# A chunk's rows of an attention and mixture-of-experts kernel: one product per pair of heads over all 128 array rows, or one per head in each half of the array rows

## The chip, the cores and the metric

The kernel runs on one core of a Trainium2 chip. The metric is the device time of one execution in microseconds (us), and smaller is better. A core has TensorE for matmuls (PE in the profile; its weight loader is PEld), VectorE (DVE), ScalarE (ACT), GpSimd (POOL) and SyncE (SP), which here issues most DMAs. TensorE multiplies a stationary operand, loaded into its array of 128 rows by 128 columns, with a moving operand whose columns stream past it. The array can be used as a whole or as smaller tiles, such as four of 64x64.

## The reference

Windowed attention for 8 batches, 8 heads, 576 positions and a head size of 64, and then a mixture of 8 experts with one expert per token:

```python
scores = scale * np.matmul(q, k.transpose(0, 1, 3, 2))
mask = (rel >= 0) & (rel < window)                       # window = 128
scores = np.where(mask, scores + bias[None], -1000000000.0)
attn = np.exp(scores - max); attn = attn / (sum + 1e-09)
x = (attn @ v) as rows of 512 per token                  # 4608 tokens
...
expert_idx = np.argmax(x @ w_gate, axis=1)               # gate: softmax's largest
out[mask] = gate_w[mask, None] * (np.maximum(xe @ w1[e], 0.0) @ w2[e])
```

All inputs and outputs are fp32. The experts' inner size is 1024.

## The kernel before

The program has two stages. The attention stage (`attention`, from line 36) goes through 36 chunks of 128 query positions each; it fills the first 200 us or so. The MoE stage (`moe_static`, line 769) gathers each expert's tokens and runs the two layers in sums of fp32r products.

A chunk is worked in these parts, which `do` (line 288) calls by a number `k`:

- `scores` (line 156), twice, for four heads each: the bias goes into two PSUM banks as bf16 matmuls (line 167), and q times k is added in fp32 (line 176). Both run in 64x64 tiles: rows are two heads, columns two halves of the queries.
- `weigh` (line 184): VectorE folds the window and takes the maxima (lines 189 and 192), ScalarE takes exponentials with their sums (line 198).
- `transposes` (line 207), twice: four fp32 transposes of 128x128 by TensorE (line 211), a copy to SBUF by ScalarE (line 213) and two masks by GpSimd (lines 221 and 223).
- `av` (line 226), twice: weights times v (line 239), in 128x64 tiles, the two heads of a pair in the two column halves; in a chunk that spans two batches a part runs in 64x64 tiles. The result is x transposed: 128 partitions are the two heads of a pair, 64 dimensions each, and the columns are 128 queries. ScalarE copies it to SBUF as `xT` (line 286).
- `rows` (line 244), once: turns x back to rows of tokens and takes the gate's logits in the same products. For each of the four pairs of heads one fp32 matmul (line 249) has `xT[:, p, :]` as the stationary operand, 128x128, and 144 columns of the constant `iw_sb` as the moving one: a 128x128 identity, and 16 columns with the pair's gate weights, 8 per head, zero where the head is the other one. The result goes to `r_ps`, two PSUM banks, two pairs in each. VectorE then multiplies by the reciprocal sums of the softmax, first the gate columns and then the rest (line 254), into `x_sb`; `done` (line 1214) adds up the logits (line 1220) and writes the rows to DRAM (line 1227).

An fp32 matmul appears in the trace as two passes, each with a weight load of its own. So the 144 row products of the program are 288 passes at line 249.

The order is written out by hand: `LAGS` gives each part of a chunk a step (4 steps per chunk), `rank` orders the parts in a step, and for the first 152 steps the engines execute in exactly that order. In a common step the second transposes of one chunk, the rows of an earlier one and the first transposes of a later one follow each other on TensorE.

`route` (line 464) works out where each token goes in its expert's list. Its small bf16 matmuls put their results in columns of `r_ps` that the rows leave free; `spare` (line 458) gives them out. The constant `iw` is built on the host (`consts`, line 1256) and loaded once (line 150).

Of the kernel before, what the change touches and what calls it, by code (L numbers as in the profile page):

```python
# [9 lines left out]
F32 = mybir.dt.float32  # L10
# [9 lines left out]
B, H, S, D = 8, 8, 576, 64  # L20
N, DM, E, F = B * S, H * D, 8, 1024
QB = 32
NP = H // 2
XW = 128 + 2 * E
SUB = 129
PITCH = 4 * SUB

# [8 lines left out]
def attention(ctx, tc, st, qT, kT, v, iw, load_c2, chunk_done, chunks, begun):  # L36
    nc = tc.nc
    const = ctx.enter_context(tc.tile_pool(name="a_const", bufs=1))
# [7 lines left out]
    ps_r = ctx.enter_context(tc.tile_pool(name="ps_r", bufs=1, space=PSUM))  # L46
# [54 lines left out]
    def make_masks():  # L101
        nc.gpsimd.memset(mask_sb, 1.0)
        for n, h in ((0, slice(0, 128)), (1, slice(0, 64)), (1, slice(64, 128))):
            nc.gpsimd.affine_select(out=mask_sb[h, n, :], in_=mask_sb[h, n, :], pattern=[[-1, 128]], base=0, channel_multiplier=1,
                                    compare_op=ALU.is_ge, fill=0.0)
    iw_sb = const.tile([128, NP, XW], F32, name="iw_sb")
    ident = st["ident"]

    warm = const.tile([128, 512], BF16, name="warm")
# [46 lines left out]
    def scores(subs, g):  # L156
        m, tail = subs[0][1] // 4, is_tail(subs)
        lo, hi = (0 if m else 128), (192 if tail else 256)
        s_ps = score_banks()
        halves = lambda c: slice(64 * c, 64 * c + 64)  # L160
        span = lambda a: (0, 192) if tail else (max(lo, 64 * a), 192 + 64 * a)
        for a in range(2):
            x0, x1 = span(a) if m else (lo, hi)
            t0 = x0 if tail else x0 - 64 * a
            for c in range(2):
                h = halves(c)
                nc.tensor.matmul(out=s_ps[halves(a), c, :, x0:x1], lhsT=eye_sb[h], rhs=bias_sb[h, 2 * g:2 * g + 2, t0:t0 + x1 - x0],
                                 start=True, stop=False)
        for n in range(2):
            for a in range(2):  # L170
                b, qs = subs[2 * a][0], slice(0, 64) if tail else halves(a)
                x0, x1 = span(a)
                k0 = 128 * (m - 1) + x0
                for c in range(2):
                    h = halves(c)
                    nc.tensor.matmul(
                        out=s_ps[halves(a), c, n, x0:x1], lhsT=blocks["q", b, m][h, 2 * g + n, qs],
                        rhs=batch[b][h, 2 * g + n, k0:k0 + x1 - x0], start=False, stop=n == 1)
        return s_ps, m, tail, lo, hi

    def guard(rsum):
        nc.gpsimd.tensor_tensor(out=rsum, in0=rsum, in1=eps_sb, op=ALU.add)
# [61 lines left out]
    def rows(ch, subs, xT, rsum):  # L244
        rinv = small.tile([128, H], F32, name="rinv")
        nc.vector.reciprocal(out=rinv, in_=rsum)
        st["r_ps"] = r_ps = ps_r.tile([128, NP, 256], F32, name="r_ps")
        for p in range(NP):
            nc.tensor.matmul(out=r_ps[:, p, 0:XW], lhsT=xT[:, p, :], rhs=iw_sb[:, p, :], start=True, stop=True)  # L249
        x_sb = xp.tile([128, NP, XW], F32, name="x_sb")  # L250
        for lo, n in ((128, E), (0, D)):
            cols = slice(lo, lo + 2 * n)
            split = lambda ap: ap[:, :, cols].rearrange("q p (c x) -> q p c x", c=2)
            nc.vector.tensor_tensor(
                out=split(x_sb), in0=split(r_ps),
                in1=rinv.rearrange("q (p c) -> q p c", c=2).unsqueeze(3).to_broadcast([128, NP, 2, n]), op=ALU.mult)
        chunk_done(ch, subs, x_sb)

# [2 lines left out]
    for ch, subs in enumerate(chunks):  # L261
        for b, i in subs:
            k = (b, i // 4)
# [6 lines left out]
    for b in range(1, B):  # L270
        at = 4 * next(ch for ch, subs in enumerate(chunks) if any(x == b for x, _ in subs))
# [10 lines left out]
    live, pes, sums, pTs, xTs, xps, second = {}, {}, {}, {}, {}, {}, {}  # L282

    def copy_x(ch):
        xTs[ch] = xp.tile([128, NP, 128], F32, name="xT", bufs=3)
        nc.scalar.copy(out=xTs[ch], in_=xps.pop(ch))

    def do(k, ch):
        if k == 9:
            return copy_x(ch)  # L290
        if k > 10:
            h = slice(4 * k - 44, 4 * k - 40)
            nc.vector.tensor_reduce(out=sums[ch][:, h], in_=pes[ch][:, h, :], axis=AX.X, op=ALU.add)
            return guard(sums[ch]) if k == 12 else None
        if k == 10:
            exps = second.pop(ch)
            exps((0,))
            copy_x(ch - 2)
            return exps((1,))
        subs = chunks[ch]  # L300
        if k in (0, 4):
            if k == 0:
                pes[ch] = pp.tile([128, H, 128], F32, name="pe")
                sums[ch] = small.tile([128, H], F32, name="rsum", bufs=8)
            live[ch] = scores(subs, k // 4)
        elif k in (2, 5):
            second[ch] = weigh(k // 3, pes[ch], sums[ch], *live.pop(ch), later=k == 5 and ch in SPLIT, add=ch not in SUMS)
        elif k == 1:
            pTs[ch] = ptp.tile([128, 2, H, 128], F32, name="pT")
            transposes(subs, 0, pes[ch], pTs[ch])  # L310
        elif k == 3:
            rows(ch, subs, xTs.pop(ch), sums.pop(ch))
        elif k == 6:
            transposes(subs, 1, pes[ch] if ch in SUMS else pes.pop(ch), pTs[ch])
        elif k == 7:
            xps[ch] = bank() if ch else ps_r.tile([128, NP, 256], F32, name="r_ps")[:, :, 0:128]
            av(subs, pTs[ch], xps[ch], range(NP // 2))
        else:
            av(subs, pTs.pop(ch), xps[ch], range(NP // 2, NP))
            if len(lags(ch)) < 10 and ch + 2 not in SPLIT:  # L320
                copy_x(ch)
# [136 lines left out]
def spare(st, k, n):  # L458
    if st["step"] >= FREE_T:
        return st["bank"]()[:, k, 0:n]  # L460
    return st["r_ps"][:, k, XW:XW + n]


def route(tc, st, lg, c0, G, groups):
# [65 lines left out]
    for k, n in enumerate(("tokh", "tokl")):  # L530
        nc.vector.tensor_tensor(out=rr[:, :, k, :], in0=eq,
                                in1=st[n][:, c0:c0 + G].unsqueeze(2).to_broadcast(sc3), op=ALU.mult)
    yield
    ip = spare(st, 1, E * TT)
    for g in range(G):
        for k in range(2):
# [132 lines left out]
def split_rows(tc, st, g, x_ps, xh, xl, gate):  # L669
    nc = tc.nc  # L670
    for d in range(4):
        nc.tensor.transpose(out=x_ps[:, d, :], in_=g[:, SUB * d:SUB * d + 128], identity=st["ident"])  # L672
    x_ps = x_ps[:, :, 0:xh.shape[2]]
# [14 lines left out]
def gather_parts(tc, st, g, idx, paced=False):  # L688
    parts = st["xd"][:, :].rearrange("t (a x) -> (t a) x", x=SUB)
    for s in range(4):  # L690
# [364 lines left out]
def moe_overflow(ctx, tc, st, w12, out):  # L1055
# [6 lines left out]
    with tc.For_i(0, n, 1) as i:  # L1062
# [15 lines left out]
        for f in range(8):  # L1078
            nc.sync.dma_start(out=w[:, f, :], in_=w12[bass.ds(e, 1), f].rearrange("o p c -> (o p) c"))
        g = op.tile([128, 4, SUB], F32, name="o_xg")  # L1080
        gather_parts(tc, st, g, idx4[:, :, 0:1])
# [112 lines left out]
def attn_moe_kernel(ctx, tc, qT, kT, v, c2, iw, w12, out):  # L1194
# [9 lines left out]
    with ExitStack() as actx:  # L1204
# [9 lines left out]
        def done(ch, subs, x_sb):  # L1214
            c0, G = next((c, n) for c, n in GROUPS if c <= ch < c + n)
            g = ch - c0
            if g == 0:
                lgs["lg"] = lgp.tile([128, G, E], F32, name="lg")
            lg = lgs["lg"]
            nc.vector.tensor_reduce(out=lg[:, g, :], in_=x_sb[:, :, 128:XW].rearrange("q p (c e) -> q e p c", c=2),  # L1220
                                    axis=AX.XY, op=ALU.add)
            for lo in (0, 2):
                if lo == 2 and subs[0][0] == subs[2][0]:
# [3 lines left out]
                nc.sync.dma_start(out=st["xd"][t0:t0 + n].rearrange("t (p x) -> t p x", p=NP),  # L1227
                                  in_=x_sb[QB * lo:QB * lo + n, :, 0:SUB])
            if g == G - 1:
# [26 lines left out]
def consts(moe_w_gate, moe_w1, moe_w2):  # L1256
    back = np.zeros((128, N // 128), np.int64)
    for ch, subs in enumerate(make_chunks()):
        for jj, (b, i) in enumerate(subs):
            back[QB * jj:QB * jj + QB, ch] = N - (b * S + QB * i + np.arange(QB))  # L1260
    wg = moe_w_gate.reshape(NP, 128, E).transpose(1, 0, 2)
    gate = np.zeros((128, NP, 2, E), wg.dtype)
    for c in range(2):
        gate[64 * c:64 * c + 64, :, c] = wg[64 * c:64 * c + 64]
    iw = np.concatenate([np.broadcast_to(np.eye(128, dtype=wg.dtype)[:, None], (128, NP, 128)), gate.reshape(128, NP, 2 * E)], axis=-1)
    parts = dict(ident=np.eye(128), seq=np.broadcast_to(np.arange(MAXOV), (128, MAXOV)), prof=np.broadcast_to(CAPS, (128, E)), rev=np.broadcast_to(np.arange(E, 0, -1), (128, E)), tokh=-64 * (back // 64), tokl=-(back % 64),
                 i128=np.broadcast_to(np.arange(128), (128, 128)), grp=np.arange(128)[:, None] // 32)
    c2 = np.concatenate([np.asarray(parts[n], np.float32) for n, _ in CONSTS], axis=1)
    w1 = moe_w1.reshape(E, 4, 4, 32, 8, 128).transpose(0, 4, 1, 3, 2, 5).reshape(E, 8, 128, 512)
    plain = moe_w1.reshape(E, 4, 128, 8, 128).transpose(0, 3, 2, 1, 4).reshape(E, 8, 128, 512)  # L1270
    w2 = moe_w2.reshape(E, 8, 128, DM)
    w12 = np.concatenate([np.concatenate([w1, w2], axis=-1), np.concatenate([plain, w2], axis=-1)])
    return dict(c2=c2, iw=iw, w12=np.ascontiguousarray(w12))
# [20 lines left out]
```

## Time and profile before

| | us |
|---|---|
| median of 3 runs | 647.56 |
| lowest and highest | 647.05, 647.61 |
| the profiled execution's own time | 646.91 |
| its span, first to last instruction | 645.2 |
| matmul passes of the rows (line 249) | 288, from 22.3 to 216.8 |

The granted TensorE clock was 0.998 of full speed over the span. How to read the views:

- A group of instructions is shown by line, engine, operation, output and inputs by name, and size: "128*64" ahead of a matmul's shapes is the rows and columns of the array that it uses, "128x144" the output's partitions and columns.
- In a timeline a row has the start in us, the time from the group's first start to its last end, the group, how many instructions, and in brackets the idle time ahead and what ended it. Matmuls overlap: the length that the trace gives for one is a latency, and the distance between starts is the pace.
- "issue" as what ended a wait means that the engine waited for nothing that the profile shows.

### The profile page before, as it was taken

What the parts mean: (1) busy time and instruction counts of PE and PEld (TensorE: products, weight loads), DVE (VectorE), ACT (ScalarE), POOL (GpSimd) and SP (SyncE); (2) the same over time, 40 slices, a digit from 0 to 9 for tenths busy, and PEclk for the clock granted to TensorE, in tenths of its full rate; (3) what the DMA queues carried; (4) which work ended last, traced back from release to release, by engine and by line L of the source; (5) the groups of instructions that cost most, each with busy time, mean ns of one, the idle gap of its engine ahead of it and who ended that gap; (6) DMA issues with size and microseconds to landing.
All of it is one profiled execution on the core that took longest, in us unless ns stands there. A gap on an engine that the chain in (4) does not pass through costs nothing.

```text
span 645.2 us, 15063 instructions
## 1 busy us (share of the span) xinstructions
PE 632.1 (98%) x5681; PEld 540.2 (84%) x5681; DVE 390.9 (61%) x978; ACT 314.1 (49%) x947; POOL 299.2 (46%) x414
## 2 busy tenths in 40 slices
PE   8999999999998999999999999999999999999995
PEld 4888888888887988888988898898898888888884
DVE  6578888969898785545544654555455355346411
ACT  5878889888867324433333334334233333424311
POOL 5534657769446040166236707633660660561202
PEclk9999999999999999999999999999999999999999
DMA  9958998988734263372534325333442542534101
GB/s 312 301 153 216 220 260 237 217 258 240 193 69 103 54 196 98 130 273 75 186 128 151 108 78 183 113 94 139 142 122 83 165 122 87 185 107 143 65 0 62
DMA packets 57645, 97.90 MB, mean 152 GB/s; under 512 B 11669, under 2 KB 31765, under 8 KB 56674
## 3 DMA queue, kind: packets, MB, share of 16 engines
q1 hardware_dynamic: 49090, 76.89, 39.9%
q0 software_dynamic: 8336, 19.76, 10.6%
q8 instruction: 46, 0.75, 0.5%
q10 hardware_dynamic: 144, 0.26, 0.2%
q14 instruction: 29, 0.24, 0.1%
HBM read 77.91 MB, written 18.98 MB: 150 GB/s over the span
## 4 chain that ended last, share of the span: by engine, by line
PE 67%; ACT 0%; DVE 0%; issue 0%; POOLq 0%; POOL 0%; ACTq 0%
PE y_ps L907 32%; PE l_ps L711 30%; PE s_ps L711 2%; PE x_ps L672 1%; PE b_ps L239 1%; PE y_ps L867 1%; PE r_ps L249 0%; PE x_ps L867 0%; ACT pe L198 0%; POOLq L1060 0%; PE l_ps L683 0%; DVE y L915 0%; DVE nmax L192 0%; ACT e_xh L674 0%; DVE s_ps L189 0%
## 5 line engine op out<-in xcount | busy, mean ns | idle before, releaser
L714 ACT ACTIVATE hh<-l_ps 128x336 fp32r<-128x336 f32 (+7 forms) x104 | 45.9, 446 | 203.4 <-PE l_ps L711 176.9
L718 DVE SCALAR_TENSOR_TENSOR hl<-l_ps,hh 128x336 fp32r<-128x336 f32 (+7 forms) x104 | 51.7, 501 | 152.4 <-ACT hh L714 137.5
L691 POOL DMA_INDIRECT xg<-xd,od_idx x112 | 114.8, 1025 | 35.1 <-issue 34.8
L198 ACT ACTIVATE pe<-s_ps,nmax 128x128 f32<-128x128 f32 x288 | 102.9, 382 | 33.7 <-DVE nmax L192 27.0
L907 PE MATMUL y_ps<-wh,hh 128*128 128x512 f32 (+5 forms) x280 | 111.0, 397 | 0.0
L907 PE MATMUL y_ps<-wh,hl 128*128 128x512 f32 (+5 forms) x280 | 110.4, 394 | 0.0
L907 PE MATMUL y_ps<-wl,hh 128*128 128x512 f32 (+5 forms) x280 | 110.3, 394 | 0.0
L895 POOL DMA_INDIRECT out<-y,od_pidx x33 | 34.6, 1049 | 147.8 <-ACT y L913 141.2
L999 DVE TENSOR_TENSOR wl<-w_raw,wh 128x512 fp32r<-128x512 f32 x114 | 73.9, 690 | 32.0 <-ACT wh L995 27.4
L711 PE MATMUL l_ps<-xh,wh 128*128 128x304 f32 (+9 forms) x416 | 81.8, 318 | 0.3 <-DVE hl L718 0.3
L711 PE MATMUL l_ps<-xl,wh 128*128 128x304 f32 (+9 forms) x416 | 81.1, 316 | 0.3 <-issue 0.3
L711 PE MATMUL l_ps<-xh,wl 128*128 128x304 f32 (+9 forms) x416 | 81.0, 317 | 0.0
L711 PEld LDWEIGHTS l_ps<-xh,wh 128*128 128x128 f32 x416 | 68.0, 189 | 9.0 <-issue 1.2
L711 PEld LDWEIGHTS l_ps<-xl,wh 128*128 128x128 f32 x416 | 66.3, 189 | 2.3 <-issue 0.6
L711 PEld LDWEIGHTS l_ps<-xh,wl 128*128 128x128 f32 x416 | 66.4, 189 | 1.9
L239 PE MATMUL b_ps<-pT,v_sb 128*64 128x128 f32 (+2 forms) x1136 | 65.4, 265 | 0.4 <-ACT pT L213 0.4
L239 PEld LDWEIGHTS b_ps<-pT,v_sb 128*64 128x64 f32 (+1 forms) x1136 | 56.1, 136 | 10.0 <-issue 4.9
L907 PEld LDWEIGHTS y_ps<-wh,hl 128*128 128x128 f32 (+5 forms) x280 | 51.4, 184 | 13.7 <-DVE hl L718 0.2
L907 PEld LDWEIGHTS y_ps<-wl,hh 128*128 128x128 f32 (+5 forms) x280 | 51.5, 184 | 11.3
L907 PEld LDWEIGHTS y_ps<-wh,hh 128*128 128x128 f32 (+5 forms) x280 | 51.4, 184 | 10.4 <-ACT hh L714 0.5
L995 ACT CAST wh<-w_raw 128x1024 fp32r<-128x1024 f32 x57 | 59.5, 1044 | 1.0 <-DMA w_raw<-w 1.0
L198 ACT ACTIVATION_READ_ACCUMULATOR pe<-s_ps,nmax 128x1 f32 x272 | 59.6, 219 | 0.0
(225 smaller groups left out, 958.2 us busy)
## 6 DMA issues: line engine op xcount, KB each, us to landing
w_raw<-w SPq DMA_DIRECT2D x64, 512.0 KB
q_sb<-qT SPq DMA_DIRECT2D x39, 256.0 KB
xd<-x_sb SPq DMA_DIRECT2D x32, 258.0 KB
v_sb<-v SPq DMA_DIRECT2D x32, 256.0 KB
k_sb<-kT SPq DMA_DIRECT2D x7, 1152.0 KB
w_n<-w SPq DMA_DIRECT2D x4, 1024.0 KB
xg<-xd,od_idx POOLq DMA_INDIRECT x112
xd<-x_sb SPq DMA_DIRECT2D x8, 129.0 KB
```

The lines of the kernel that those rows point to most:

```text
L198: nc.scalar.activation(out=pe[:, h, :], in_=s_ps[:, c, n, lo:lo + 128], func=AF.Exp, bias=nmax[:, 2 * c + n:2 * c + n + 1], scale=1.0, **( ...
L239: nc.tensor.matmul(out=x_ps[64 * c:64 * c + 64, p, q], lhsT=blocks["v", b, m - 1 + kb][0:kk, D * h:D * h + D], rhs=pT[0:kk, kb, h, q], sta ...
L672: nc.tensor.transpose(out=x_ps[:, d, :], in_=g[:, SUB * d:SUB * d + 128], identity=st["ident"])
L691: ins = tc.nc.gpsimd.indirect_dma_start(out=g[:, s], out_offset=None, in_=parts, in_offset=bass.IndirectOffsetOnAxis(ap=idx[:, s], axis=0),)
L711: nc.tensor.matmul(out=ps, lhsT=a[:, 128 * d:128 * d + 128], rhs=b[:, d], start=(k == 0), stop=(k == 11))
L714: nc.scalar.activation(out=hh, in_=ps, func=AF.Relu)
L718: nc.vector.scalar_tensor_tensor(out=hl, in0=ps, scalar=0.0, in1=hh.bitcast(F32), op0=ALU.max, op1=ALU.subtract)
L867: nc.tensor.matmul(out=ps[m * g:m * g + n], lhsT=hrs[p][:, f, :], rhs=w2s[p][:, f % 4, w * g:w * g + w], start=f == 0, stop=f == 7)
L895: ins = nc.gpsimd.indirect_dma_start(**kw).ins
L907: nc.tensor.matmul(out=ys[t][0:n], lhsT=a[:, tl], rhs=b[:, 512:1024], start=(f == 0 and k == 0), stop=(f == 7 and k == 2))
L995: keep(tc, nc.scalar.copy(out=wh, in_=raw))
L999: keep(tc, eng.tensor_tensor(out=wl[:, sl], in0=raw[:, sl], in1=wh.bitcast(F32)[:, sl], op=ALU.subtract))
```

## The change

`rows` makes eight matmuls in place of four. For each pair and each of its two heads, 64 partitions of `xT` are the stationary operand (64 rows by 128 columns) and 64 partitions of `iw_sb` the moving one, now with 72 columns: a 64x64 identity and the 8 gate weights. So each head has a product in its own half of the array's rows, in a 64x128 tile. The outputs of the first heads go to one PSUM bank of `r_ps`, those of the second heads to the other. VectorE's two multiplications read the new places and write `x_sb` as before. `iw` has 72 columns per pair instead of 144. `spare` gives out other free columns of the same banks.

```diff
+RW = D + E
...
-    iw_sb = const.tile([128, NP, XW], F32, name="iw_sb")
+    iw_sb = const.tile([128, NP, RW], F32, name="iw_sb")
...
-        st["r_ps"] = r_ps = ps_r.tile([128, NP, 256], F32, name="r_ps")
+        st["r_ps"] = r_ps = ps_r.tile([128, 2, 512], F32, name="r_ps")
+        r4 = r_ps[:, :, 0:NP * RW].rearrange("q c (p x) -> q p c x", p=NP)
         for p in range(NP):
-            nc.tensor.matmul(out=r_ps[:, p, 0:XW], lhsT=xT[:, p, :], rhs=iw_sb[:, p, :], start=True, stop=True)
+            for c in range(2):
+                h = slice(64 * c, 64 * c + 64)
+                nc.tensor.matmul(out=r4[:, p, c, :], lhsT=xT[h, p, :], rhs=iw_sb[h, p, :], start=True, stop=True)
         x_sb = xp.tile([128, NP, XW], F32, name="x_sb")
-        for lo, n in ((128, E), (0, D)):
-            cols = slice(lo, lo + 2 * n)
-            split = lambda ap: ap[:, :, cols].rearrange("q p (c x) -> q p c x", c=2)
+        for lo, at, n in ((128, D, E), (0, 0, D)):
             nc.vector.tensor_tensor(
-                out=split(x_sb), in0=split(r_ps),
+                out=x_sb[:, :, lo:lo + 2 * n].rearrange("q p (c x) -> q p c x", c=2), in0=r4[:, :, :, at:at + n],
                 in1=rinv.rearrange("q (p c) -> q p c", c=2).unsqueeze(3).to_broadcast([128, NP, 2, n]), op=ALU.mult)
...
-    return st["r_ps"][:, k, XW:XW + n]
+    return st["r_ps"][:, k // 2, NP * RW + 64 * (k % 2):NP * RW + 64 * (k % 2) + n]
...
-    gate = np.zeros((128, NP, 2, E), wg.dtype)
-    for c in range(2):
-        gate[64 * c:64 * c + 64, :, c] = wg[64 * c:64 * c + 64]
-    iw = np.concatenate([np.broadcast_to(np.eye(128, dtype=wg.dtype)[:, None], (128, NP, 128)), gate.reshape(128, NP, 2 * E)], axis=-1)
+    eye = np.tile(np.eye(D, dtype=wg.dtype), (2, 1))
+    iw = np.concatenate([np.broadcast_to(eye[:, None], (128, NP, D)), wg], axis=-1)
```

TensorE's list before the change, in the middle of the attention stage (bias and scores into `s_ps`, transposes into `b_ps`, the rows into `r_ps`, then weights times v):

```order
L167 LDWEIGHTS eye_sb
L167 MATMUL s_ps<-bias_sb,eye_sb 64x2x192
L176 MATMUL s_ps<-k_sb,q_sb 64x192 x8
L211 MATMUL b_ps<-c_sb,pe 128x128 x4
L249 MATMUL r_ps<-iw_sb,xT 128x144 x4
L211 MATMUL b_ps<-c_sb,pe 128x128 x4
L239 MATMUL b_ps<-pT,v_sb 64x64 x16
```

And at the same place in the changed kernel, whose lines are numbered a little higher:

```order
L168 LDWEIGHTS eye_sb
L168 MATMUL s_ps<-bias_sb,eye_sb 64x2x192
L177 MATMUL s_ps<-k_sb,q_sb 64x192 x8
L212 MATMUL b_ps<-c_sb,pe 128x128 x4
L253 MATMUL r_ps<-iw_sb,xT 128x72 x8
L212 MATMUL b_ps<-c_sb,pe 128x128 x4
L240 MATMUL b_ps<-pT,v_sb 64x64 x16
```

Nothing moves: eight products of 72 columns stand where four of 144 stood, between the same transposes. That is so in all 36 places; on the other engines only the load of `iw` is smaller.

More of the change, by code (lines that the diff above doesn't have):

```diff
@@ L315, in do @@
         elif k == 7:
-            xps[ch] = bank() if ch else ps_r.tile([128, NP, 256], F32, name="r_ps")[:, :, 0:128]
+            xps[ch] = bank() if ch else ps_r.tile([128, 2, 512], F32, name="r_ps").rearrange("p c (a x) -> p (c a) x", a=2)[:, :, 0:128]
             av(subs, pTs[ch], xps[ch], range(NP // 2))
```

## The prediction

> **What bounds the kernel now.** I read the page first, then busy time over the long even part of the attention stage, then what TensorE waits for there. The page's head and its first part:
>
> ```profile
> span 645.2 us, 15063 instructions
> ...
> PE 632.1 (98%) x5681; PEld 540.2 (84%) x5681; DVE 390.9 (61%) x978; ACT 314.1 (49%) x947; POOL 299.2 (46%) x414
> ```
>
> TensorE is at 98%, but ends of matmuls are modelled, so this alone proves little. Busy time by engine in two stretches (PE, PEld, DVE, ACT and POOL, then granted clock, DMA share and GB/s):
>
> ```profile
> 0.00:20.00 20.00, 16.39 (x219) 10.23 (x221) 13.91 (x29) 13.10 (x47) 12.06 (x36) 1.00 0.93 330
> 40.00:198.00 158.00, 157.68 (x2544) 131.08 (x2543) 134.13 (x356) 131.74 (x553) 98.38 (x159) 1.00 0.78 206
> ```
>
> From 40 to 198 us VectorE and ScalarE each do about 133 us in 158, or 85%. Whether TensorE truly never waits is seen at its weight loader, which runs ahead of the matmuls. The largest waits of TensorE and of the loader from 20 to 198 us (total us, times, longest):
>
> ```profile
> PE r_ps L537 <- DVE x_sb L254: 0.3, 1, 0.3
> ...
> PEld b_ps L211 <- issue: 5.6, 22, 0.3
> PEld L167 <- issue: 4.7, 28, 0.2
> PEld b_ps L239 <- issue: 4.4, 19, 0.3
> PEld b_ps L239 <- POOL pT L221: 2.9, 11, 0.3
> ```
>
> TensorE itself waits once, for 0.3 us. The loader's waits are short, of one length, mostly for nothing that the profile shows, and they stand at changes of tile shape. So this stage is TensorE's work in order, and what a chunk's rows cost there goes into the span. There are 36 of them (288 passes are 36 x 8):
>
> ```profile
> L249 PE MATMUL r_ps<-iw_sb,xT x288: 285/286/391, 22.3 to 216.8; 128*128 128x144 f32 x144
> ```
>
> Their 286 ns is a latency; passes start much closer. The pace is the distance between groups, and one chunk's TensorE stream shows it (start, length, group, tile rows*columns, times):
>
> ```profile
> 105.79 0.66 PE L211 MATMUL b_ps<-c_sb,pe 128*128 128x128 f32 x4
> 106.29 1.15 PE L249 MATMUL r_ps<-iw_sb,xT 128*128 128x144 f32 x8
> 107.27 0.60 PE L211 MATMUL b_ps<-c_sb,pe 128*128 128x128 f32 x4
> 107.80 0.36 PE L167 MATMUL s_ps<-bias_sb,eye_sb 64*64 64x384 bf16 x4
> 107.99 0.82 PE L176 MATMUL s_ps<-k_sb,q_sb 64*64 64x192 f32 x16
> 108.74 0.44 PE L239 MATMUL b_ps<-pT,v_sb 128*64 128x128 f32 x4
> ```
>
> The rows take 107.27 - 106.29 = 0.98 us: 8 passes (each fp32 matmul makes two) at 0.1225 us, or 0.85 ns a column.
>
> **The change: columns streamed.** The new code streams 8 matmuls of 72 columns, 16 passes, in two row halves with a bank each. If the halves run side by side, 8 slots of 72 x 0.85 = 0.061 us replace 8 of 0.1225. Quarters of the array do run side by side: L176's 16 passes of 192 columns would need 16 x 192 x 0.85 ns = 2.6 us in turns, and take 108.74 - 107.99 = 0.75.
>
> **Weight loads.** Every pass loads its own weights, here 128 columns of xT, and the change keeps 128 columns per load while it doubles the loads from 8 to 16. The cost of such a load is seen where the stream is too short to hide it, in the 42-column products of L683 (loader, then matmuls):
>
> ```profile
> 232.44 0.97 PEld L683 LDWEIGHTS l_ps<-od_idx,sel 128*128 128x128 f32 x8
> 233.34 0.19 PEld L907 LDWEIGHTS y_ps<-wh,e_hl 128*128 128x128 f32 x1
> ...
> 232.55 0.98 PE L683 MATMUL l_ps<-od_idx,sel 128*128 128x42 f32 x8
> ```
>
> Eight loads take 233.34 - 232.44 = 0.90 us, 0.112 each, although 42 columns stream in 0.036. At 144 columns the load hides under the stream (0.112 under 0.1225); at 72 it doesn't (0.112 over 0.061). So a slot costs 0.112 us, if both halves load at once. That loads overlap is seen in a chunk with 64-column streams:
>
> ```profile
> 102.17 0.48 PEld L176 LDWEIGHTS s_ps<-k_sb,q_sb 64*64 64x64 f32 x16
> ...
> L176 PEld LDWEIGHTS s_ps<-k_sb,q_sb 64*64 64x64 f32 x1024 | 35.9, 133 | 2.5
> ```
>
> The last of 16 loads begins 0.48 - 0.13 = 0.35 us after the first. A 64-column load should take half of 0.112; in turns the 15 ahead of it would need 15 x 0.056 = 0.84 us, and with only column halves in parallel 7 x 0.056 = 0.39. So row halves overlap as well, by a narrow margin. The last pair is followed by no load of its own, which saves 0.112 - 0.061 = 0.05. New rows: 8 x 0.112 - 0.05 = 0.85 us.
>
> The Trainium skill, "TensorE: Matmul & The Clock Gate", section "LDWEIGHTS (loading the stationary operand)", says that a load lasts its columns over 1.2 ns and that its rows don't matter: an estimate of 107 ns here; the trace's 0.112 agrees. By it the sum would be 8 x 0.005 = 0.04 us a chunk lower.
>
> **Changes of tile shape.** Rows now run in tiles of 64x128; the transposes on both sides (L211) run in 128x128. Two changes of shape are added per chunk. What one costs is read from four transposes of 128 columns, which last 4 x 128 x 0.85 = 0.436 us undisturbed, as here between others of their shape:
>
> ```profile
> 202.88 0.60 PE L672 MATMUL s_ps<-c_sb,e_xg 128*128 128x128 f32 x4
> 203.31 1.15 PE L249 MATMUL r_ps<-iw_sb,xT 128*128 128x144 f32 x8
> ```
>
> That is 0.43. Just after a change, 106.29 - 105.79 = 0.50: 0.06 more. Just ahead of one, 107.80 - 107.27 = 0.53: 0.09 more. Together 0.16 per change. Changing rows alone is no cheaper:
>
> ```profile
> 41.96 1.09 PE L239 MATMUL b_ps<-pT,v_sb 128*64 128x128 f32 x16
> 42.99 0.36 PE L167 MATMUL s_ps<-bias_sb,eye_sb 64*64 64x384 bf16 x4
> ```
>
> Here 128*64 lies between two stretches of 64*64, and 8 slots of 0.109 = 0.87 us take 1.03: 0.16 for coming in and going out. Two changes a chunk cost 0.32.
>
> On the same point the Trainium skill, "TensorEngine Tiling (Array Packing)", section "Key Properties", says that changing the tiling mode drains TensorE. It gives no price; the rows above agree, with 0.16 us.
>
> **The sum.** Per chunk 0.85 + 0.32 - 0.98 = +0.19 us; the two-decimal rows leave 0.02 either way, and I take 0.18. No row shows a 64x128 tile, so I bound the shape-bound part from both sides: streams alone, 8 x 0.061 + 0.32 - 0.98 = -0.17, and loads wholly in turns, 16 x 0.112 - 0.05 + 0.32 - 0.98 = +1.08. I stay at +0.18, since the row nearest in kind (same weights' width, short stream) is L683. Over 36 chunks: 6.5 us.
>
> Some of it falls into waits that are there anyway, near the end of the stage:
>
> ```profile
> 204.29 0.60 PE L211 MATMUL b_ps<-c_sb,pe 128*128 128x128 f32 x4
> 205.40 0.66 PE L211 MATMUL b_ps<-c_sb,pe 128*128 128x128 f32 x4 [0.51 <-ACT pT L213]
> 206.47 0.77 PE L239 MATMUL b_ps<-pT,v_sb 128*64 128x128 f32 x10 [0.41 <-ACT pT L213]
> ```
>
> Two or three chunks' 0.18 can vanish here: -0.5 us.
>
> **What else changes.** VectorE's two products (L254) read as many elements as before, from two banks:
>
> ```profile
> L254 DVE TENSOR_TENSOR x_sb<-r_ps,rinv x72: 224/453/682, 23.9 to 217.3; 128x64 f32<-128x64 f32 x36, 128x512 f32<-128x512 f32 x36
> ```
>
> I take no change; VectorE's 15% of free time in the stretch covers a few tens of ns either way, and without that cover 36 times 0.04 would be 1.4 us. The constant iw halves:
>
> ```profile
> iw_sb<-iw SPq DMA_DIRECT2D x1, 288.0 KB
> ...
> PE s_ps L167 <- ACT pe L198: 1.6, 3, 0.9
> ```
>
> The 144 KB less is 0.45 us at the 330 GB/s of the first 20 us. TensorE's largest early wait is for exponentials, not for a transfer, so I take 0, with -0.45 as the bound. The order of all instructions on every engine is otherwise that of before, so no queue is passed; the MoE stage starts later by what the rows add and is itself unchanged.
>
> Total: 6.5 - 0.5 = +6.0 us. The profiled execution took 646.91 us, its span 645.2; it would take 652.9. The median of the three timed runs is 647.56, 0.65 above it; on that the forecast is 653.5. Runs lie between 647.05 and 647.61, so about 0.2%, 1.3 us, is what a measurement of this kernel can tell from no change.
>
> **Rivals.** (1) *Streams set the pace*: loads of 64 rows hide after all, and a slot costs 0.061. Then -0.17 x 36 = -6.1 us, of which the other engines at 85% let nearly all through: 641.5. For it: 64-column streams in quarters keep their own pace. Against: there the load has 64 columns too, so it was never the longer of the two. It decides as soon as a 128-column load takes under 0.061. By the Trainium skill, "TensorEngine Tiling (Array Packing)", "Theoretical Speedup", a contracted dimension of 64 is worth up to 2x; the trace bears that out only where loads are as short as the streams. Chance 0.09.
>
> (2) *No drain between 64x128 and 128x128*: the 0.32 goes, 0.85 - 0.98 = -0.13, -4.7 us: 642.9. Against: the row-only change at L239. Chance 0.06.
>
> (3) *Halves stream in turns*: 16 x 0.061 + 0.32 - 0.98 = +0.32, 11.5 us: 659. Against: L176. Chance 0.06.
>
> (4) *Halves load in turns*: +1.08, 38.9 us: 686. For it: the margin of 0.35 against 0.39 is narrow, and quarters aren't halves. Chance 0.05.
>
> (5) *The change does nothing to the time*: the extra is covered by the loader's waits, 647.6. Against: those waits are the drains themselves. Chance 0.04.
>
> **How the numbers follow.** The forecast has 0.70. Faster: (1) and (2), 0.15. Within 0.2%: (5), 0.04. Slower: the forecast, (3) and (4), 0.81. The predicted time is the forecast's, 653.5. Its own range, with 0.12 to 0.22 a chunk, is 651.5 to 655.5. The range that holds 8 in 10 takes in (3) and (5) with it, 0.80: 647.5 to 659.
>
> **What would show it.** In the profile of the changed kernel: the row products' first start to the next transposes at 0.95 to 1.15 us instead of 0.98 (slots of 0.112, then the drain of 0.09), the transposes behind them 0.06 longer, and from the last transposes ahead of them 0.09 more. The loader shows new waits for "issue" of 0.17 to 0.28 us at rows and at the transposes after them, up to 36 of each; chunks follow each other 0.18 us later, and the MoE stage is as long as before. I am wrong if the rows' slots come at 0.06 (rival 1), if no wait appears at rows (2), or if the starts of a pair lie 0.06 or 0.11 apart with 16 in a line (3, 4).

## The result, and the profile after

| | before | changed |
|---|---|---|
| median of 5 runs, us | 647.54 | 653.96 |
| lowest and highest | 647.05, 647.61 | 652.96, 654.90 |
| profiled execution: time, span | 646.91, 645.2 | 654.45, 652.6 |

The change makes the kernel slower: 1.0102 times the time before, with a 95% interval of 1.0087 to 1.0117, or 6.4 us between the medians. The forecast was 653.5.

The page's head and first part for the changed kernel:

```profile
span 652.6 us, 15658 instructions
...
PE 639.8 (98%) x5969; PEld 539.2 (83%) x5969; DVE 392.6 (60%) x978; ACT 314.8 (48%) x947; POOL 299.0 (46%) x414
```

TensorE has 288 passes more (5969 against 5681), which are the doubled rows. The other three engines have the same instructions and the same busy time within 1.7 us. TensorE is at 98% as before: this share tells nothing of what changed. The even part of the attention stage, as before (PE, PEld, DVE, ACT, POOL, then granted clock, DMA share and GB/s):

```profile
40.00:198.00 158.00, 157.76 (x2684) 125.62 (x2681) 130.54 (x338) 127.37 (x532) 95.45 (x155) 1.00 0.74 202
```

In the same 158 us VectorE now gets through 338 instructions where it had done 356, and ScalarE through 532 instead of 553. Their busy time over the whole run is nearly the same, so they were not slowed; they wait for TensorE a little more. One chunk's stream on TensorE, in the place of the one shown before:

```profile
108.71 0.66 PE L212 MATMUL b_ps<-c_sb,pe 128*128 128x128 f32 x4
109.30 1.11 PE L253 MATMUL r_ps<-iw_sb,xT 64*128 64x72 f32 x16
110.35 0.65 PE L212 MATMUL b_ps<-c_sb,pe 128*128 128x128 f32 x4
110.93 0.36 PE L168 MATMUL s_ps<-bias_sb,eye_sb 64*64 64x384 bf16 x4
```

Three distances between starts tell what happened. From the first transposes to the rows: 0.59 us, where it was 0.50. From the rows to the next transposes: 1.05, where it was 0.98. From those to the bias: 0.58, where it was 0.53. Together +0.21 us a chunk. The loader's waits from 20 to 198 us (total us, times, longest):

```profile
PEld b_ps L212 <- issue: 4.9, 19, 0.3
...
PEld r_ps L253 <- issue: 3.3, 19, 0.3
```

The second line is new (before, the loader waited at the rows once in this stretch): the loader now waits there too, 0.17 us each time on average, for nothing that the profile shows.

The trace's starts within the rows, in ns from one pass to the next, show the slots (changed kernel, the rows at 109.30):

```
last transpose to first pass 203 | 7 160 6 105 7 105 7 105 6 105 7 105 7 105 6 | to the next transpose 203, to its second 164
```

The two halves of a pair start 6 or 7 ns apart, so they run side by side. Pair follows pair at 111 or 112 ns, and at 167 the first time. In the kernel before, the same list (the rows at 106.29) reads 109 | 125 122 123 122 123 122 123 | 122, 109.

The time of a chunk, from its first row pass to that of the next chunk, is 0.21 us longer than before in 27 of the 35 steps between chunks; in the steps to chunks 31, 32 and 33 it is the same to 0.01. The first row pass of chunk 35 comes 6.56 us later than before (222.47 against 215.91). From there to the end 0.8 us more is added in the profiled execution. The second layer's products, in before and then in the changed kernel (their last figures ahead of the shapes are first and last start):

```profile
L907 PE MATMUL y_ps<-wl,hh x280: 387/393/405, 241.2 to 637.8; 128*128 128x512 f32 x123, 128*78 128x512 f32 x5, 128*106 128x512 f32 x4, 128*102 128x512 f32 x4
```

```profile
L909 PE MATMUL y_ps<-wl,hh x280: 387/393/404, 247.9 to 644.7; 128*128 128x512 f32 x123, 128*78 128x512 f32 x5, 128*106 128x512 f32 x4, 128*102 128x512 f32 x4
```

First start to last start is 396.6 us and 396.8 us. From the last start to the end of the span it is 7.4 and 7.9 us; no line here says why. Nearly the whole loss stands in the attention stage.

### The profile page after: what moved, and what is told of

The parts are those of the page before. It is cut to its first block, busy times and chain, and to the rows that moved or that the text cites. A ratio compares the mean times of both kernels' runs of the same rounds, so it can differ in the third digit from the quotient of the medians.

```text
span 652.6 us, 15658 instructions
## 1 busy us (share of the span) xinstructions
PE 639.8 (98%) x5969; PEld 539.2 (83%) x5969; DVE 392.6 (60%) x978; ACT 314.8 (48%) x947; POOL 299.0 (46%) x414
## 4 chain that ended last, share of the span: by engine, by line
PE 56%; issue 8%; POOL 2%; ACT 1%; DVE 0%; POOLq 0%; ACTq 0%
PE y_ps L909 26%; PE l_ps L713 26%; PE s_ps L713 2%; POOL out L897 1%; POOL xg L693 1%; PE x_ps L674 1%; PE b_ps L240 1%; PE y_ps L869 1%; PE r_ps L253 0%; PE x_ps L869 0%; ACT pe L199 0%; POOLq L961 0%; ACT hh L716 0%; ACT wh L997 0%; PE l_ps L685 0%
```

## The experiments

The theory is that of the prediction: a row slot costs the weight load of 128 columns (0.112 us), whatever the number of rows and however short the stream, and two changes of tile shape per chunk cost a little over 0.3 us. The first rival puts the loss into the stream (columns times 0.85 ns), a second into halves that take turns. All experiments are variants of the changed kernel, unless said otherwise; ratios are to the kernel before in the same series.

### A wider stream under the same load

```diff
-RW = D + E
+RW = 100
```

The constant is filled up with zeros, so each of the 8 products streams 100 columns instead of 72.

> The changed kernel with the moving operand of the rows widened from 72 to 100 columns per head; the 28 added columns are zeros and nobody reads them. Theory (a slot of two row products is set by its weight loads of 128 columns, 0.112 us): the stream of 100 columns, 0.085 us, still hides under the load, slots stay at 0.112 and the time at the changed kernel's 654.0, within 1 us. Rival (the halves stream in turns, and 0.112 is near two streams of 0.061 by chance): slots of 2 x 0.085 = 0.17, 8 x 0.058 = 0.46 us more per chunk, 36 times: 669 to 671.

Measured: 654.89 us (654.49 to 655.42), ratio 1.0113 (1.0096 to 1.013).

```profile
109.16 0.66 PE L212 MATMUL b_ps<-c_sb,pe 128*128 128x128 f32 x4
109.75 1.14 PE L253 MATMUL r_ps<-iw_sb,xT 64*128 64x100 f32 x16
110.82 0.66 PE L212 MATMUL b_ps<-c_sb,pe 128*128 128x128 f32 x4
```

39% more columns make the rows 0.02 us longer (110.82 - 109.75 = 1.07 against 1.05), where a stream that set the pace would have added 8 x 28 x 0.85 ns = 0.19. The stream is hidden under the load.

### Whole array, no change of shape

```diff
-    iw_sb = const.tile([128, NP, RW], F32, name="iw_sb")
+    iw_sb = const.tile([128, NP, 2, RW], F32, name="iw_sb")
...
-                nc.tensor.matmul(out=r4[:, p, c, :], lhsT=xT[h, p, :], rhs=iw_sb[h, p, :], start=True, stop=True)
+                nc.tensor.matmul(out=r4[:, p, c, :], lhsT=xT[:, p, :], rhs=iw_sb[:, p, c, :], start=True, stop=True)
```

The same 8 products of 72 columns on all 128 rows, with zeros in the other head's rows of the constant. The added changes of shape are gone, and so are the halves.

> The eight products of 72 columns in tiles of the whole array, 128x128, with zeros in the other head's rows of the moving operand: as many loads as in the changed kernel, none side by side, and no change of tile shape. Theory (loads of 128 columns at 0.112 us set the pace whatever their rows): the rows take 16 x 0.112 = 1.79 us instead of 0.98, +0.81 a chunk, 29 us less 1 to 4 us that fall into waits at the end of the stage: 672 to 676. Rival (the changed kernel lost only by the changes of shape, and loads hide): 16 x 0.061 = 0.98, the time of the kernel before, 647.5.

Measured: 672.55 us (672.41 to 672.67), ratio 1.0387 (1.037 to 1.0405).

```profile
104.60 0.66 PE L212 MATMUL b_ps<-c_sb,pe 128*128 128x128 f32 x4
105.10 1.90 PE L252 MATMUL r_ps<-iw_sb,xT 128*128 128x72 f32 x16
106.84 0.60 PE L212 MATMUL b_ps<-c_sb,pe 128*128 128x128 f32 x4
107.37 0.36 PE L168 MATMUL s_ps<-bias_sb,eye_sb 64*64 64x384 bf16 x4
```

On both sides the distances are back to those of before (0.50 and 0.53), so 0.09 and 0.05 us belong to the change of shape. The 16 passes stand in one line, 111 or 112 ns apart but for the first (65), though each streams only 61 ns. That is the same slot for 128 rows as for 64 in the changed kernel. The Trainium skill, "TensorE: Matmul & The Clock Gate", section "LDWEIGHTS (loading the stationary operand)", says just this: columns count, rows don't; by its columns over 1.2 ns the slot would be 107 ns. The halves are worth 1.74 - 1.05 = 0.69 us a chunk; they do work in parallel, loads included.

### The change of shape alone

The kernel before, with one tiny product in a 64x64 tile ahead of the rows, into columns that nobody reads:

```diff
+        nc.tensor.matmul(out=r_ps[0:64, 3, XW:XW + 8], lhsT=eye_sb[0:64], rhs=bias_sb[0:64, 0, 0:8], start=True, stop=True)
         for p in range(NP):
             nc.tensor.matmul(out=r_ps[:, p, 0:XW], lhsT=xT[:, p, :], rhs=iw_sb[:, p, :], start=True, stop=True)
```

> The kernel before with one bf16 matmul of 8 columns in a 64x64 tile ahead of each chunk's rows, into columns that nobody reads: two changes of tile shape per chunk, the rows as they were. Theory (a change costs about 0.15 us: 0.09 to drain and 0.06 of a load that nothing hides): +0.25 to +0.30 a chunk, 9 to 11 us, less about 1 us in waits: 655.5 to 657.5. Rival (changes of shape cost little and the changed kernel lost by its loads): the small matmul alone, 0.03 a chunk: 648 to 649.

Measured: 657.05 us (656.48 to 657.40), ratio 1.0145 (1.0128 to 1.0162).

```profile
110.03 0.66 PE L211 MATMUL b_ps<-c_sb,pe 128*128 128x128 f32 x4
110.61 0.19 PE L248 MATMUL r_ps<-bias_sb,eye_sb 64*64 64x8 bf16 x1
110.73 1.25 PE L250 MATMUL r_ps<-iw_sb,xT 128*128 128x144 f32 x8
111.81 0.60 PE L211 MATMUL b_ps<-c_sb,pe 128*128 128x128 f32 x4
```

From the transposes to the rows it is 0.70 us, where it was 0.50, and the rows take 1.08 instead of 0.98. In the trace's ns the three distances around the tiny product are 202, 120 and 227, where there were 109 and 125: +0.315 us for two changes, with the tiny product's own time in it. Over 36 chunks this is 11.3 us; 9.4 arrive at the end. The rival's 0.03 a chunk is refuted: at most 0.16 us a change, and not much less, is paid outside of the rows' new tile shape too. Rival 2 of the prediction, no drain between 64x128 and 128x128, is refuted by the changed kernel itself, with its 0.09 us ahead of the rows.

### One change of shape fewer

The rows' products are issued directly behind the scores, ahead of the first transposes, in 32 of the chunks, so that a third shape doesn't split the transposes; VectorE's part stays where it was:

```diff
+        if ch > 2 and lags(ch)[6] == 8 and lags(ch - 2)[3] == 17:
+            products(ch - 2, xTs[ch - 2])
```

> The changed kernel with the rows' products of 32 chunks issued one step earlier, between the scores (64x64) and the transposes (128x128), so that one change of shape per chunk is added and not two; VectorE's part of the rows stays in its place. Theory: 32 x 0.15 = 4.8 us less than the changed kernel: 648.5 to 650. Rival (two changes cost no more than one, or the transposes and with them the exponentials come later by the rows and cost as much): 653.5 or above.

Measured: 652.10 us (651.38 to 652.53), ratio 1.007 (1.0053 to 1.0086). That is 1.9 us faster than the changed kernel, but 2 us short of what was expected. The steps between chunks tell why: 23 of the 35 are 0.06 us longer than before, 0.15 less than in the changed kernel, as the theory has it. Four others are longer by 0.61, 0.63, 0.78 and 1.01, those to chunks 3, 12, 21 and 30 (two steps near the end, of -1.22 and +1.36, nearly cancel). TensorE's waits from 20 to 216 us:

```profile
PE b_ps L240 <- ACT pT L214: 2.2, 5, 0.6
PE r_ps L548 <- DVE x_sb L263: 0.5, 1, 0.5
```

Where products of weights and v follow the transposes directly, the rows used to stand between and gave ScalarE time for the copy. In the new place they don't, and TensorE waits up to 0.6 us. The saving of a change of shape is real, but in these four steps 2.8 of the 4.8 us that 32 times 0.15 make are given back. Each of the four has one such place: the first product of weights and v starts 0.60 to 0.92 us behind the last transpose, where it was 0.20. That is 2.1 of the 2.8.

### Quarters: loads of 64 columns

```diff
-            for c in range(2):
-                h = slice(64 * c, 64 * c + 64)
-                nc.tensor.matmul(out=r4[:, p, c, :], lhsT=xT[h, p, :], rhs=iw_sb[h, p, :], start=True, stop=True)
+            for a in range(2):
+                for c in range(2):
+                    h, q = slice(64 * c, 64 * c + 64), slice(64 * a, 64 * a + 64)
+                    nc.tensor.matmul(out=r4[q, p, c, :], lhsT=xT[h, p, q], rhs=iw_sb[h, p, :], start=True, stop=True)
```

The rows run in four 64x64 tiles, 16 products of 72 columns. A load has 64 columns now, half as long, and the stream of 0.061 us should set the slot.

> The changed kernel with each head's product split once more, by halves of the 128 queries: 16 products of 72 columns in 64x64 tiles, 32 passes, at the same place between the transposes. Theory (loads set the pace as far as they are longer than the streams): a load of 64 columns, 0.056 us, hides under a stream of 0.061; four tiles at a time make 8 slots of 0.061 to 0.065, 0.51 us, and the two changes of shape stay at 0.30: 0.51 + 0.30 - 0.98 = -0.17 a chunk against the kernel before, 6 us: 641 to 643. Rival (the number of instructions sets the pace: 32 loads and 32 passes at 0.028 us each pair or more are as long as the 0.89 of the changed kernel): no faster than the changed kernel, 654 or above.

Measured: 647.35 us (644.40 to 652.87, 12 runs), ratio 1.0005 (0.9983 to 1.0026): the time of before, with a spread four times as wide (before: 646.30 to 648.34 in 23 runs). The expected gain did not come. What the theory says of the rows did (the profiled execution took 650.86 us, 3.5 more than the median of these runs):

```profile
107.91 0.66 PE L212 MATMUL b_ps<-c_sb,pe 128*128 128x128 f32 x4
108.50 0.73 PE L254 MATMUL r_ps<-iw_sb,xT 64*64 64x72 f32 x32
109.16 0.66 PE L212 MATMUL b_ps<-c_sb,pe 128*128 128x128 f32 x4
109.74 0.36 PE L168 MATMUL s_ps<-bias_sb,eye_sb 64*64 64x384 bf16 x4
```

The rows take 0.66 us where they took 1.05 in the changed kernel and 0.98 before; the slots are 0.062 or 0.063 behind the first. 15 of the 35 steps between chunks are 0.17 or 0.18 us shorter than before, which is rival 1's -0.17 to the digit. Over 36 chunks that would be -6.1 us at the last chunk; the trace has +3.16 there. So 9.3 us were lost elsewhere in this execution; at the median it would be about 6. TensorE's waits from 20 to 216 us (the head of the list):

```profile
PE s_ps L177 <- issue: 1.5, 1, 1.5
PE r_ps L254 <- issue: 1.4, 1, 1.4
PE b_ps L212 <- ACT pT L214: 1.2, 2, 0.7
PE b_ps L240 <- issue: 0.9, 2, 0.7
PE b_ps L212 <- ACT xT L289: 0.8, 3, 0.3
PE r_ps L540 <- DVE x_sb L257: 0.6, 1, 0.6
```

Two kinds are mixed here. The waits for xT, pT and x_sb are for other engines. Those of the transposes for pT were there before (1.3 us); TensorE's own wait for xT is new, and the one for x_sb was 0.3: with a shorter chunk TensorE runs into ScalarE and VectorE. The waits for "issue" are something else, single pauses within a run of equal matmuls, on nothing that the profile names:

```profile
57.07 0.71 PE L254 MATMUL r_ps<-iw_sb,xT 64*64 64x72 f32 x27
59.23 0.34 PE L254 MATMUL r_ps<-iw_sb,xT 64*64 64x72 f32 x5 [1.45 <-issue]
```

From 20 to 205 us there are six distances of over 0.29 us between two passes of one group without a wait on a semaphore, and none in the kernel before or the changed one. I numbered TensorE's instructions (loads, matmuls and the few others, as the trace has them) and put beside each pause the last packet of TensorE's code that landed ahead of its end:

```
pause from   us      group          instruction, and modulo 256    code packet landed   us to the end of the pause
 26.29      0.38   weights times v       706   194                    25.12               1.56
 32.62      1.82   scores                962   194                    33.11               1.33
 57.56      1.67   rows                 1985   193                    57.84               1.39
133.81      0.98   weights times v      5057   193                   133.36               1.43
140.58      0.47   scores               5313   193                   139.64               1.41
146.93      0.49   weights times v      5570   194                   145.96               1.47
```

All six fall on the same place modulo 256, 193 or 194, in three different groups, and all end 1.3 to 1.6 us after a packet has landed. The packets are those of this line of the page (before: 46 packets, 0.75 MB):

```profile
q8 instruction: 52, 0.85, 0.6%
```

0.85 MB in 52 packets is 16 KB each. TensorE has 13206 instructions in this kernel, 12054 in the changed one and 11474 in before, and this queue 52, 48 and 46 packets; that is 256 instructions of 64 bytes to a packet, and the instructions that were added are all TensorE's. The place, the same in three kinds of group, and the landing ahead of each end leave a want of code as the cause that fits; what passes in the 1.3 us and more between landing and end is not shown. The Trainium skill, "Runtime: NRT & Kernel Launch", section "Instruction fetch mechanics", says that code comes in blocks of 256 instructions, the next one fetched while the current one is executed, and that crossing to a new block is "mostly hidden". The trace agrees on the block; that the crossing is hidden holds for before and not here. Between 20 and 200 us TensorE reaches a new block every 7.8 us on average in before, every 7.4 in the changed kernel and every 6.3 in this one, and the next block had landed 5.0, 5.0 and 2.9 us ahead (means; the least are 2.2, 1.5 and 1.3). Packets that come late are not new: counted from the moment when TensorE reaches a block, the packet of the next one starts up to 4.7 us later in before, 5.4 in the changed kernel and 5.4 here (means 1.7, 1.4 and 2.3). With a block every 7.8 or 7.4 us no pause followed, and with one every 6.3 six did. In this kernel eight of 29 packets start over 3.4 us late, those of the six pauses among them; in the 3 us behind each such edge the 16 DMA engines are full (a share of 1.0 on average, against 0.77 for the other 21). That speaks for packets that stand behind other transfers, but no run tests it. The six pauses are worth 4.9 us beyond an ordinary distance of 0.16. The other 4.4 us of the 9.3 are left for waits on other engines; TensorE's list names 3.0 us of such waits, where it named 2.0 in before, so most of this rest is not shown piece by piece.

### Quarters next to the scores

The last two edits together. The rows run in 64x64 tiles directly behind the scores, which have that shape already, so that nearly all added changes of shape go as well.

> The same 64x64 products, in 32 chunks issued one step earlier, straight behind the scores that run in the same tile shape, so that no change of shape is added. Theory: 0.51 - 0.98 = -0.47 a chunk, 15 to 16 us, of which new waits give some back (with the rows gone from between the transposes, the second product of weights and v waits for ScalarE's copy in some steps, 2 us where only the place was changed) and VectorE and ScalarE, 85% busy before, come close to their limit: 633 to 637. Rival (the other engines take over at once): no better than with the products in their old place, 641 to 643.

Measured: 648.61 us (645.91 to 651.87, 11 runs), ratio 1.0023 (1.0006 to 1.0041). A miss by over 11 us. TensorE's waits from 20 to 216 us:

```profile
PE s_ps L177 <- issue: 3.3, 2, 3.1
PE b_ps L240 <- ACT pT L214: 1.4, 4, 0.4
PE b_ps L212 <- ACT xT L296: 1.3, 4, 0.5
PE r_ps L549 <- DVE x_sb L264: 0.9, 1, 0.9
```

The same two causes are at work. Four pauses without a semaphore come at 193 or 194 modulo 256 again, 4.2 us together beyond an ordinary distance, the longest of 3.46 us at 31.38 (instruction 961). This one has a consequence of its own, seen in busy time by stretch (the three figures at the end are granted clock, DMA share, GB/s):

```profile
20.00:30.00 10.00, 10.00 (x226) 8.47 (x224) 5.82 (x15) 8.37 (x39) 5.28 (x11) 1.00 0.92 235
30.00:40.00 10.00, 6.86 (x104) 5.86 (x102) 2.68 (x7) 4.70 (x22) 3.70 (x8) 0.70 0.49 165
```

The clock granted to TensorE falls from 1.00 to 0.70 on average over these 10 us, and just behind the pause the rows' slots take 0.12 us, twice the 0.062. By the Trainium skill, "TensorE: Matmul & The Clock Gate", section "Part 1: The HAM clock gate (the "warmup" mystery)", the clock goes to half after an idle window of about 3.4 us. The trace shows it sooner: the clock is at half from 33.95 to 40.78 us, and at 33.95 the last pass ahead of the pause had ended 2.3 us ago. None of the shorter pauses, up to 1.8 us, did it. From 40 to 198 us the steps between chunks are up to 0.7 us shorter than before, but 8 of the 27 are 0.15 to 0.9 longer; three of these hold a pause for code. At the last chunk the rows come 1.96 us later than before, where -0.47 in 32 chunks and -0.17 in 4 would be 15.7 us earlier. Of these 17.7 us the pauses are 4.2, and the step over the slow clock, to chunk 3, is 2.3 longer than it should be. The other 11 or so are left for waits on other engines, of which TensorE's list names 5.2. No version here beats the kernel before.

## Why the prediction was right

**The bound.** "This stage is TensorE's work in order" held: the loss is in TensorE's distances alone, at 0.21 us in 27 of 35 steps, and the MoE stage took 396.8 us for 396.6.

**The slot.** 0.112 was forecast from another group's loads and 0.111 to 0.112 was measured. The wider stream shows that the stream is hidden (+0.02 us a chunk for 39% more columns), the whole-array version that the number of rows doesn't matter. Rivals 3 and 4, halves that stream or load in turns, are refuted by starts 6 or 7 ns apart, and by the 0.69 us that the halves save against the whole array. Rival 1 failed as the prediction said, on the load of 128 columns; with 64 columns a slot of 0.062, near its 0.061, appears.

**The changes of shape.** +0.09 ahead of the rows and +0.055 at the first of the transposes behind them were measured as forecast, and the tiny product gives 0.315 for two changes and itself. Also the first pair within the rows comes 0.055 later than the others, the uncovered load that was counted there. With 0.09 more behind the rows the two changes make 0.295 us, where 0.32 was taken.

**The term that failed: "The last pair is followed by no load of its own, which saves 0.112 - 0.061 = 0.05."** It doesn't. From the last pair to the next transpose the trace has 202 or 203 ns, not the 153 of this term. Put beside other groups, the distance out of a group at a change of shape is the group's own slot plus 0.09, and a slot set by loads counts in full even where no load of the group follows:

```
out of                       slot    distance to the next shape
rows in quarters             0.062   0.153
transposes                   0.109   0.202
rows in halves               0.112   0.202
scores, 192 columns          0.163   0.253
```

The wider stream, with 100 columns, has 0.202 as well, so it is the slot that counts and not the stream. A chunk costs 8 x 0.112 + 0.295 - 0.98 = +0.21 us, and 36 of them 7.6 us instead of 6.5; half of what this term had wrong is hidden by the 0.295 (the prediction's sum was 0.19, and it took 0.18). Why the last pass holds its slot isn't shown by these runs.

**The other mis-sized term** is what vanishes in waits that were there anyway: 0.5 us was taken, about 1.0 is measured (7.6 - 6.6). The steps to chunks 31, 32 and 33 lost nothing, and the one to chunk 15 only 0.05. The two errors partly cancel, which is luck: +6.6 at the end of the stage against +6.0 forecast, and +6.4 between the medians.

**VectorE and the constant.** Both cost nothing, as taken. In the changed kernel:

```profile
L256 DVE TENSOR_TENSOR x_sb<-r_ps,rinv 128x512 f32<-128x512 f32 x36 | 24.5, 681 | 0.0
...
L256 DVE TENSOR_TENSOR x_sb<-r_ps,rinv 128x64 f32<-128x64 f32 x36 | 8.1, 225 | 7.6 <-PE r_ps L253 5.1
```

681 and 225 ns, where the longest and the shortest had been 682 and 224.

**A remark that is doubtful.** Of rival 1 the prediction said that "the other engines at 85% let nearly all through". The quarters bear on it: in the profiled execution 4.4 us, of the 6.1 that the rows saved, are left for waits for other engines, besides the 4.9 lost to code. A mean of 85% over the stage says nothing of the slack in single chunks. No quarter run came under 644.40, so 641.5 was too low for a slot of that size in this kernel; how much of that rival 1's own code, with half as many instructions in the rows, would have lost is not shown.

## What to carry to other kernels

By these runs, splitting a product over row halves pays only if the stream is what sets the slot: compare columns loaded with columns streamed first, since halving the rows leaves the load as long as it was (0.112 us here for 64 rows and for 128). In this kernel every change of tile shape that was put between other work cost about 0.15 us more, and the group's last slot counted in full. And when an edit shortens the path, look for what is next in single chunks, not in means: here ScalarE, VectorE and TensorE's own code were all close behind.

## What was not expected of the hardware

- TensorE can run dry of instructions. With 64 of them for a chunk's rows in 0.66 us, a new block of 256 came due every 6.3 us instead of 7.8, and TensorE stood still six times, for 0.4 to 1.8 us, each time at the same place modulo 256 (four times in the last version, once for 3.5 us).
- Within a pause of 3.5 us the granted clock fell to half and stayed there for 6.8 us: 0.70 on average over 10 us, and row slots of 0.12 us for 0.062.
- A slot that is set by a weight load longer than the stream counts in full at the end of a group too: 0.202 us out of the halves, where 0.153 was expected.
